# 32-column tiles for attention values and row sums, a bank of their own for the sums, and a new placing of the surrounding matmuls

## The chip, the cores and the metric

The kernel runs on one core of one Trainium2 chip. The metric is device time in microseconds (us) of one execution. The median of several executions is quoted, with the lowest and highest. Engines are named as in the profile: PE (matmuls), PEld (weight loads, overlapping PE), DVE (VectorE), ACT (ScalarE), POOL (GpSimd), SP (SyncE). Where the text says "wait", the next instruction in the engine's order could not start yet. An instruction that is ready can also stand behind others that the program issued before it on its engine; the profile before shows a case of 1.5 us.

## The reference, cut to what matters

Attention over 8 batches of 8 heads (576 tokens, 64 channels per head, 16 extra "beacon" keys that everybody sees, otherwise causal), then a gated feed-forward block on the result:

```python
# q, k, v: (8, 8, 576, 64); beacon_k, beacon_v: (8, 8, 16, 64)
scores = scale * q @ concat(beacon_k, k).T        # causal on the 576 own keys
a = exp(scores - max); a /= a.sum(-1)
x = (a @ concat(beacon_v, v))                     # -> (4608, 512), heads side by side
out = (gelu(x @ w_gate) * (x @ w_val)) @ w_out    # 512 -> 1536 -> 512
```

## The kernel before: the parts that matter

Heads go in pairs (4 pairs per batch, m = 0 to 3). For each pair, scores come in four chunks: a and b, then c and d, each into one of two "scores" tiles of PSUM (`psum_s`, two buffers), from where ACT takes the exponential. "Attend" multiplies the exponentials with the values, and with a block of ones for the row sums. The feed-forward gates of a batch follow, as one block of 96 matmuls; the output matmuls (48 per batch, index u) of the *previous* batch are spread between the attention steps of the next one, to give PE something to do while ACT works. (The feed-forward runs in nine chunks of 512 tokens; the last two come after the last batch.) Twelve output matmuls accumulate one output tile, which DVE then copies out of PSUM.

```python
psum_s: 2 buffers of 2 banks;  psum_x: 1 buffer of 3 banks;  psum_o: 1 buffer of 1 bank

def attend(b, m, t, wide=False):         # two column tiles: head 0 and head 1, 64 columns each
    ...
    for w, (ps, base, split) in enumerate(x_of[i]):      # w=0: values, w=1: sums
        for q0, q1 in ...:
            for hi in range(2):
                mm(ps[64*hi : 64*hi+64, base+q0 : base+q1],
                   ones[0:kr, :] if w else v_sb[0:kr, t, 2*m+hi, :],
                   expT[0:kr, hi, e0 : e0+q1-q0], ...)

def normalize(b, m, by_act=False, direct=False):
    ...
    act(x_sb, x_ps, ACT.Copy)                             # values out of PSUM (not if direct)
    keep(nc.vector.transpose(zT_sb, z_ps))                # 128 x 576
    keep(nc.vector.reciprocal(r_sb, ...))                 # 128 x 18
    keep(nc.vector.transpose(rec_sb, r_sb spread))        # 128 x 576
    keep(nc.vector.tensor_tensor(out=xT_sb[...], in0=x_sb, in1=rec_sb, op=ALU.mult))

def out_mms(ci, u0, u1, wide):
    for u in range(u0, u1):
        ti, fi = divmod(u, 12)
        if fi == 0:       # a new output tile: tile 0 in psum_x, tiles 1 to 3 in the one bank psum_o
            o_ps = psum_x.tile(...) if wide(ti) else psum_o.tile(...)
        mm(o_ps, ...)
        if fi == 11:
            keep(nc.vector.tensor_copy(o_sb[:, ti, :], o_ps)); ...   # and the store

# one batch, from the second on (o(n): the next n output matmuls of the batch before)
o(6);  ab(0);  o(10);  cd(0);  o(8)
for m in 1, 2, 3:
    ab(m);  av(m - 1);  cd(m);  o(6 if m < 3 else 5)      # av = attend, then normalize
av(3);  o(7)
... 96 gate matmuls ...
```

`keep` pins an instruction to its place in the program's order on its engine.

The softmax here doesn't subtract the row's maximum and nothing guards it: scores larger than these inputs give would overflow.

## Time and profile before

398.44 us, median of 3 runs (398.13 to 399.09).

| | before |
|---|---|
| span in the profile | 396.2 us |
| PE busy | 382.3 us, 97% |
| ACT / DVE / POOL busy | 51% / 48% / 39% |
| granted PE clock | full (1.00) |
| one steady batch | 42.2 us |

From the page of the kernel before, part 1, and the two rows of part 2 for PE and its clock (the span in 40 slices, each digit tenths):

```profile
PE 382.3 (97%) x3046; PEld 185.9 (47%) x3046; DVE 190.5 (48%) x304; ACT 202.2 (51%) x280; POOL 156.3 (39%) x277
...
PE   3889999999999999999999999999999999999996
...
PEclk9999999999999999999999999999999999999999
```

Only the first slices and the last are not full. Busy time alone would not prove that PE is the limit, but the list of what PE waited for does (columns: who waited, for whom, total us, how often, longest us). These are all of its lines:

```profile
PE t_ps L167 <- DMA qk_103<-in_q_dram: 4.4, 1, 4.4
PE s_ps L155 <- DVE qkT L183: 1.5, 1, 1.5
PE x_ps L155 <- DVE zT_sb L304: 1.1, 1, 1.1
PE s_ps L155 <- ACT expT L158: 1.0, 2, 0.8
PE gv_ps L155 <- DVE xT_sb L312: 0.8, 1, 0.8
PE x_ps L155 <- DVE x_sb L297: 0.4, 1, 0.4
PE t_ps L167 <- DVE qkT L183: 0.4, 2, 0.2
PE t_ps L167 <- DMA qk_103<-in_k_dram: 0.2, 1, 0.2
PE s_ps L155 <- DMA qkT<-k_sb_94: 0.2, 1, 0.2
```

Nearly all of it is in the first 32 us. After that the kernel is a stream of PE work with no hole worth speaking of.

The timeline of the kernel before around the end of an output tile, DVE and the next output matmul only (columns: start us, duration us, engine, line, operation, tiles, shapes, count):

```profile
111.79 0.78 DVE L307 STREAM_TRANSPOSE rec_sb<-r_sb 128x576 f32<-128x576 f32 x1
...
112.60 0.76 DVE L312 TENSOR_TENSOR xT_sb<-x_sb,rec_sb 128x576 bf16<-128x576 f32 x1
...
113.28 0.68 DVE L364 COPY o_sb<-o_ps 128x512 f32<-128x512 f32 x1
...
114.37 0.61 PE L155 MATMUL o_ps<-wo_sb,hT_sb 128*128 128x512 bf16 x2
```

The output tile that is copied at 113.28 got its last matmul from 111.43 to about 111.8. The copy began 1.5 us after that, behind the transposes and the multiply of a normalization that the program issued before it. In this kernel that did no harm, because the group of output matmuls ended with that tile, and the next one started at 114.37, 0.4 us after the copy's end.

The c/d scores that follow an attend, from their start to the next output matmul (PE only):

```profile
105.78 0.60 PE L155 MATMUL s_ps<-qkT 64*128 64x464 bf16 x4
106.32 1.47 PE L155 MATMUL o_ps<-wo_sb,hT_sb 128*128 128x512 bf16 x6
```

That is 0.54 us, against 0.39 us for the c/d scores of pair 0, which have ten output matmuls before them.

### The profile page before, as it was taken

To read this page: it belongs to the slowest core of one execution; us is meant where nothing else is said; L and a number is where in the kernel's file an instruction comes from. 1 tells how busy PE (TensorE), PEld (TensorE's weight loads), DVE (VectorE), ACT (ScalarE), POOL (GpSimd) and SP (SyncE) were. 2 spreads that over 40 slices of the span, in tenths; PEclk is the share of its full clock that TensorE was granted. 3 is DMA by queue.
4 is the path that set the end of the run, shared out by engine and by line. 5 is a ranking of instruction groups with operands and counts; after the bars stand their busy time and mean duration, and the time that the engine had idled before them with its cause. 6 is when DMAs were issued, how large, how long until landed. Compare 5 with 4: busy or idle time off the path is not lost.

```text
span 396.2 us, 7413 instructions
## 1 busy us (share of the span) xinstructions
PE 382.3 (97%) x3046; PEld 185.9 (47%) x3046; DVE 190.5 (48%) x304; ACT 202.2 (51%) x280; POOL 156.3 (39%) x277
## 2 busy tenths in 40 slices
PE   3889999999999999999999999999999999999996
PEld 2464545544454445444544455444544455444442
DVE  1393654844375327642673338433754266332332
ACT  2775258634873379336843586347823793332210
POOL 8722395780369124931486047803400240000000
PEclk9999999999999999999999999999999999999999
DMA  7999998699129930996099915991032010000012
GB/s 91 180 206 204 175 132 97 68 169 121 55 36 156 141 79 30 120 156 84 29 107 162 89 55 57 163 137 58 28 89 59 34 45 32 0 0 29 28 53 106
DMA packets 139154, 36.24 MB, mean 91 GB/s; under 512 B 126832, under 2 KB 134512, under 8 KB 139120
## 3 DMA queue, kind: packets, MB, share of 16 engines
q0 software_dynamic: 103984, 19.14, 64.4%
q1 hardware_dynamic: 35136, 16.62, 19.3%
q8 instruction: 24, 0.39, 0.4%
q14 instruction: 10, 0.08, 0.1%
HBM read 38.27 MB, written 9.44 MB: 120 GB/s over the span
## 4 chain that ended last, share of the span: by engine, by line
PE 79%; DMA 8%; POOL 3%; DVE 3%; ACT 3%; issue 2%; SPq 2%; POOLq 0%; ACTq 0%
PE gv_ps L155 36%; PE o_ps L155 23%; PE x_ps L155 11%; PE s_ps L155 8%; DMA qkT<-k_sb_94 3%; DMA v_sb_98<-in_beacon_v_dram 2%; SPq L196 2%; ACT expT L158 2%; DMA k_sb_97<-in_k_dram 2%; POOL k_sb_97 L109 1%; PE t_ps L167 1%; DVE qkT L178 1%; POOL q_sb_96 L109 1%; PE w_ps L155 1%; DMA kb<-in_beacon_k_dram 1%
## 5 line engine op out<-in xcount | busy, mean ns | idle before, releaser
L158 ACT ACTIVATE ge_sb<-gv_ps 128x512 bf16<-128x512 f32 x108 | 64.5, 597 | 150.7 <-PE gv_ps L155 150.7
L340 DVE TENSOR_TENSOR hT_sb<-gv_ps,ge_sb 128x512 bf16<-128x512 f32 x108 | 74.7, 692 | 116.0 <-ACT ge_sb L158 116.0
L158 ACT ACTIVATE expT<-s_ps 128x1024 bf16<-128x1024 f32 (+3 forms) x128 | 103.9, 870 | 25.8 <-PE s_ps L155 25.7
L155 PE MATMUL gv_ps<-xT_sb,wg_sb 128*128 128x512 bf16 x432 | 112.2, 379 | 0.8 <-DVE xT_sb L312 0.8
L155 PE MATMUL gv_ps<-xT_sb,wv_sb 128*128 128x512 bf16 x432 | 112.2, 379 | 0.0
L238 POOL TENSOR_SCALAR_AFFINE_SELECT expT<-expT 128x256 bf16<-128x256 bf16 (+2 forms) x140 | 52.4, 388 | 142.2 <-ACT expT L158 142.1
L155 PE MATMUL o_ps<-wo_sb,hT_sb 128*128 128x512 bf16 x432 | 103.6, 380 | 0.0
L155 PEld LDWEIGHTS <-wv_sb 128*128 128x128 bf16 x432 | 42.3, 98 | 52.7 <-issue 2.7
L155 PEld LDWEIGHTS <-wg_sb 128*128 128x128 bf16 x432 | 41.9, 98 | 49.9
L155 PEld LDWEIGHTS <-hT_sb 128*128 128x128 bf16 x432 | 38.8, 98 | 46.6 <-issue 2.8
L364 DVE COPY o_sb<-o_ps 128x512 f32<-128x512 f32 x36 | 24.7, 687 | 37.9 <-PE o_ps L155 37.9
L155 PE MATMUL s_ps<-qkT 64*128 64x80 bf16 (+5 forms) x384 | 39.1, 294 | 2.7 <-DVE qkT L183 1.5
L155 PE MATMUL x_ps<-expT,ones 128*64 128x432 bf16 (+1 forms) x558 | 41.2, 243 | 0.0
L304 DVE STREAM_TRANSPOSE zT_sb<-x_ps 128x576 f32<-128x576 f32 x29 | 22.7, 781 | 29.9 <-ACT x_sb L158 29.9
L155 PEld LDWEIGHTS <-qkT 64*128 64x128 bf16 x384 | 14.8, 96 | 30.4 <-issue 21.8
L155 PEld LDWEIGHTS <-ones 128*64 128x64 bf16 (+1 forms) x578 | 23.2, 110 | 4.6
L307 DVE STREAM_TRANSPOSE rec_sb<-r_sb 128x576 f32<-128x576 f32 x29 | 22.6, 778 | 1.0
L155 PE MATMUL x_ps<-expT,v_sb_95 128*64 128x80 bf16 (+5 forms) x270 | 21.5, 245 | 1.5 <-DVE zT_sb L304 1.1
L155 PE MATMUL x_ps<-expT,v_sb_98 128*64 128x80 bf16 (+5 forms) x288 | 22.8, 246 | 0.0
L109 POOL DMA_DIRECT2D v_sb_98<-in_v_dram x20 | 17.0, 868 | 11.9 <-DMA wv_sb<-in_moe_w_val_dram 3.7
L109 POOL DMA_DIRECT2D v_sb_95<-in_v_dram x20 | 17.0, 889 | 2.5 <-DMA k_sb_94<-in_k_dram 2.3
L312 DVE TENSOR_TENSOR xT_sb<-x_sb,rec_sb 128x576 bf16<-128x576 f32 x23 | 17.4, 758 | 0.9
(51 smaller groups left out, 190.9 us busy)
## 6 DMA issues: line engine op xcount, KB each, us to landing
out_dram<-o_sb SPq DMA_DIRECT2D x36, 256.0 KB, 2.0
v_sb_95<-in_v_dram POOLq DMA_DIRECT2D x12, 128.0 KB, 7.9
wg_sb<-in_moe_w_gate_dram POOLq DMA_DIRECT2D x3, 512.0 KB, 11.6
wv_sb<-in_moe_w_val_dram POOLq DMA_DIRECT2D x3, 512.0 KB, 13.3
wo_sb<-in_moe_w_out_dram POOLq DMA_DIRECT2D x1, 1536.0 KB, 23.5
v_sb_98<-in_v_dram POOLq DMA_DIRECT2D x12, 128.0 KB, 10.6
q_sb_93<-in_q_dram POOLq DMA_DIRECT2D x12, 128.0 KB, 4.2
q_sb_96<-in_q_dram POOLq DMA_DIRECT2D x12, 128.0 KB, 4.2
```

Of the source, the lines that this page charges most:

```text
L109: keep(nc.gpsimd.dma_start(out=out_ap, in_=in_ap))
L155: keep(nc.tensor.matmul(out_ap, lhsT, rhs, start=start, stop=stop, **kw))
L158: keep(nc.scalar.activation(out_ap, in_ap, func, **kw))
L167: keep(nc.tensor.transpose(out_ap, in_ap, ident[0:n, 0:n]))
L178: nc.vector.tensor_copy(qkT[:, m, :, NB:SK].rearrange("p w (t r) -> p w t r", r=6), t_ps[:, 0:2, 0:S].rearrange("p w (r t) -> p w t r", r=6),)
L196: nc.sync.dma_start_transpose(out=qkT[:, :, w, c + j * P : c + j * P + n], in_=src[0:n, j, :, :].rearrange("p h d -> p (h d)"),)
L238: nc.gpsimd.affine_select(out=d, in_=d, pattern=[[0, 2], [1, n]], compare_op=ALU.is_ge, fill=0.0, base=NB if t == 0 else 0, channel_multip ...
L304: keep(nc.vector.transpose(zT_sb, z_ps))
L307: nc.vector.transpose(rec_sb.rearrange("p (c o) -> p c o", o=32), r_sb.to_broadcast([P, S // 32, 32]))
L312: nc.vector.tensor_tensor(out=xT_sb[:, m, b * S : (b + 1) * S], in0=x_sb, in1=rec_sb, op=ALU.mult)
L340: nc.vector.tensor_tensor(out=h_of[ci][:, fi, :], in0=gv_ps[:, 1, :], in1=ge_sb, op=ALU.mult)
L364: keep(nc.vector.tensor_copy(o_sb[:, ti, :], o_ps))
```

## The change

Its intent: the row sums do not need 64 copies per head. With 32-column tiles, four tiles fit side by side in the array, so two query ranges (0 to 352 and 352 to 576) of both heads are summed at once: 960 streamed columns instead of 1664. Values use 32-column tiles too (same streamed columns), so that the shape of the array does not change within an attend; heads then interleave over groups of 32 rows, and the gate weights are loaded in that order. Sums come first and go to a bank of their own (`psum_z`), so DVE can start on them while the values still stream; the multiply reads the values from PSUM, which saves ACT the copy (0.66 us each in the trace before). The last two gate tiles are computed as a pair, gates first, so that ACT is done early. The output matmuls are placed anew.

```diff
+    psum_z = ...(name="psum_z", bufs=1, PSUM)          # one bank; psum_x shrinks to two
     def load_gate_val(i):                              # 24 weight loads instead of 6
+            for g in range(4): ... dst[32*g : 32*g+32] <- rows of (half, head) g
     def attend(b, m, x_in, by_act):
+            z_ps = psum_z.tile([P, 512], FP32, ...)
+            for t, u in Z_ORDER:                       # u: query range
+                for hi in range(2):
+                    p0 = 64 * u + 32 * hi
+                    mm(z_ps[p0 : p0 + 32, ...], ones[0 : KROWS[t], 0:32], expT[...], ...)
+        x_ps = pool.tile([P, 1024], FP32, ...)
+                for r in range(4):
+                    mm(x_ps[32*r : 32*r+32, ...], v_sb[..., 2*m + r%2, 32*(r//2) : 32*(r//2)+32],
+                       expT[..., r % 2, ...], ...)
     def normalize(b, m, by_act):
-            if not direct: act(x_sb, x_ps, ACT.Copy)
-            keep(nc.vector.transpose(zT_sb, z_ps))
-            keep(nc.vector.reciprocal(r_sb, ...))
+            keep(nc.vector.transpose(zT_sb[:, 0:w], z_ps[:, 0:w]))             # 128 x 224
+            keep(nc.vector.transpose(zT_sb[0:64, w:ZS], z_ps[0:64, w:ZS]))     # 64 x 128
+            ... four reciprocals of 64 partitions ...
     def out_mms(...):
-                    o_ps = psum_x.tile(...)             # tile 0 (tiles 1 to 3: psum_o, as before)
+                    o_ps = psum_z.tile(...)
+    def gate_val_pair(ci, f0): ... # gates of both tiles, then values of both
     # one batch
-            o(6);  ab(0);  o(10);  cd(0);  o(8)
-            for m: ab(m); av(m-1); cd(m); o(6 if m < NPAIR - 1 else 5)
-            av(3, direct=True);  o(7)
+            o(4);  ab(0);  o(6);   cd(0);  o(4)
+            for m: ab(m); av(m-1); cd(m); o(8)
+            av(3);  o(10)
```

More of the change, by code (lines that the diff above doesn't have):

```diff
@@ L38 @@
 AV_ORDER = [0, 2, 4, 1, 3]
-X0 = 16
-Z0 = X0 + S
+X0 = 512 - S_LO[4]
+ZS = 352
+Z_ORDER = [(0, 0), (0, 1), (1, 1), (1, 0), (2, 1), (2, 0), (3, 1), (4, 1)]
 QK_SCALE = 0.125
@@ L77 @@
     psum_x = ctx.enter_context(tc.tile_pool(name="psum_x", bufs=1, space=bass.MemoryType.PSUM))
+    psum_z = ctx.enter_context(tc.tile_pool(name="psum_z", bufs=1, space=bass.MemoryType.PSUM))
     psum_o = ctx.enter_context(tc.tile_pool(name="psum_o", bufs=1, space=bass.MemoryType.PSUM))
@@ L148, in load_gate_val @@
         for w, dst in ((moe_w_gate, wg_sb), (moe_w_val, wv_sb)):
-            keep(nc.gpsimd.dma_start(out=dst[:, :, fs], in_=w[:, fs].rearrange("(kk p) f -> p kk f", p=P)))
+            for g in range(4):
+                a, c = g % 2, g // 2
+                dma(
+                    dst[32 * g : 32 * g + 32, :, fs],
+                    w[:, fs].rearrange("(kk q p) f -> q p kk f", q=4, p=32)[2 * a + c],
+                )
     def load_out_w():
@@ L161, in transpose_pe @@
     def transpose_pe(b, m, pool, tag):
-        t_ps = pool.tile([P, 3 if tag == "x" else 2, 1024], BF16, name="t_ps", tag=tag)
+        t_ps = pool.tile([P, 2, 1024], BF16, name="t_ps", tag=tag)
         qk, kb = qk6[b]
@@ L251, with attend @@
     x_of = {}
-    def attend(b, m, t, wide=False):
+    def attend(b, m, x_in, by_act):
         i = b * NPAIR + m
-        if t == AV_ORDER[0]:
-            if wide:
-                x_of[i] = tuple(
-                    (psum_s.tile([P, 1024], FP32, name=name, tag="s"), 0, 512) for name in ("xs_ps", "zs_ps")
-                )
-            else:
-                x_ps = psum_x.tile([P, 1536], FP32, name="x_ps", tag="x")
-                x_of[i] = ((x_ps, X0, 512 - X0), (x_ps, Z0, 1024 - Z0))
-        expT, v_sb = exp_of[i], v_ring[b % NRING]
-        kr, first, last = KROWS[t], t == AV_ORDER[0], t == AV_ORDER[-1]
-        for w, (ps, base, split) in enumerate(x_of[i]):
-            for q0, q1 in ((S_LO[t], split), (max(split, S_LO[t]), S)):
+        expT, v_sb = exp_of[i], v_ring[b % NRING]
+        if by_act:
+            z_ps = psum_s.tile([P, 1024], FP32, name="z_ps", tag="s")
+            for t in AV_ORDER:
+                for q0, q1 in ((S_LO[t], 512), (max(512, S_LO[t]), S)):
+                    e0 = EXP_OFF[t] + q0 - S_LO[t]
+                    for r in range(4):
+                        mm(
+                            z_ps[32 * r : 32 * r + 32, q0:q1],
+                            ones[0 : KROWS[t], 0:32],
+                            expT[0 : KROWS[t], r % 2, e0 : e0 + q1 - q0],
+                            t == AV_ORDER[0],
+                            t == AV_ORDER[-1],
+                            skip_group_check=True,
+                        )
+        else:
+            z_ps = psum_z.tile([P, 512], FP32, name="z_ps", tag="z")
+            for t, u in Z_ORDER:
+                lo, end = (ZS, S) if u else (0, ZS)
+                q0 = max(lo, S_LO[t])
+                e0 = EXP_OFF[t] + q0 - S_LO[t]
+                for hi in range(2):
+                    p0 = 64 * u + 32 * hi
+                    mm(
+                        z_ps[p0 : p0 + 32, q0 - lo : end - lo],
+                        ones[0 : KROWS[t], 0:32],
+                        expT[0 : KROWS[t], hi, e0 : e0 + end - q0],
+                        t == 0,
+                        t == (4 if u else 2),
+                        skip_group_check=True,
+                    )
+        pool, tag = x_in
+        x_ps = pool.tile([P, 1024], FP32, name="x_ps", tag=tag)
+        for t in AV_ORDER:
+            for q0, q1 in ((S_LO[t], S_LO[4]), (max(S_LO[4], S_LO[t]), S)):
@@ L269, in attend @@
                 e0 = EXP_OFF[t] + q0 - S_LO[t]
-                for hi in range(2):
+                for r in range(4):
                     mm(
-                        ps[64 * hi : 64 * hi + 64, base + q0 : base + q1],
-                        ones[0:kr, :] if w else v_sb[0:kr, t, 2 * m + hi, :],
-                        expT[0:kr, hi, e0 : e0 + q1 - q0],
-                        first and (wide or not (w == 1 and q0 == 0)),
-                        last,
+                        x_ps[32 * r : 32 * r + 32, X0 + q0 : X0 + q1],
+                        v_sb[0 : KROWS[t], t, 2 * m + r % 2, 32 * (r // 2) : 32 * (r // 2) + 32],
+                        expT[0 : KROWS[t], r % 2, e0 : e0 + q1 - q0],
+                        t == AV_ORDER[0],
+                        t == AV_ORDER[-1],
@@ L277, in attend, with normalize @@
                         skip_group_check=True,
                     )
-    def normalize(b, m, by_act=False, direct=False):
+        x_of[i] = x_ps[:, X0 : X0 + S], z_ps
+    def normalize(b, m, by_act):
         i = b * NPAIR + m
-        (x_ps, xc, _), (z_ps, zc, _) = x_of.pop(i)
-        x_ps, z_ps = x_ps[:, xc : xc + S], z_ps[:, zc : zc + S]
+        x_ps, z_ps = x_of.pop(i)
         del exp_of[i]
         rec_sb = npool.tile([P, S], FP32, name="rec_sb", tag="rec_sb")
-        x_sb = x_ps
-        if not direct:
-            x_sb = npool.tile([P, S], FP32, name="x_sb", tag="x_sb")
@@ L293, in normalize @@
         if by_act:
-            ln_sb = npool.tile([P, S], FP32, name="ln_sb", tag="zT_sb")
-            act(ln_sb, z_ps, ACT.Ln)
-            if not direct:
-                keep(nc.vector.tensor_copy(x_sb, x_ps))
+            ln_sb = npool.tile([P, S], FP32, name="ln_sb", tag="ln_sb")
+            act(ln_sb, z_ps[:, 0:S], ACT.Ln)
             act(rec_sb, ln_sb, ACT.Exp, scale=-1.0)
         else:
-            zT_sb = npool.tile([P, S], FP32, name="zT_sb", tag="zT_sb")
+            zT_sb = npool.tile([P, ZS], FP32, name="zT_sb", tag="zT_sb")
@@ L301, in normalize @@
             r_sb = npool.tile([P, S // 32, 1], FP32, name="r_sb", tag="r_sb")
-            if not direct:
-                act(x_sb, x_ps, ACT.Copy)
-            keep(nc.vector.transpose(zT_sb, z_ps))
-            keep(nc.vector.reciprocal(r_sb, zT_sb.rearrange("p (c o) -> p c o", o=32)[:, :, 0:1]))
+            n, w = ZS // 32, S - ZS
+            keep(nc.vector.transpose(zT_sb[:, 0:w], z_ps[:, 0:w]))
+            keep(nc.vector.transpose(zT_sb[0:64, w:ZS], z_ps[0:64, w:ZS]))
+            z = zT_sb.rearrange("p (c o) -> p c o", o=32)[:, :, 0:1]
@@ L306, in normalize @@
+            for p in (64, 0):
+                keep(nc.vector.reciprocal(r_sb[p : p + 64, n:, :], z[64:P, 0 : w // 32, :]))
+            for p in (0, 64):
+                keep(nc.vector.reciprocal(r_sb[p : p + 64, 0:n, :], z[0:64, :, :]))
             keep(
@@ L312, in normalize @@
             nc.vector.tensor_tensor(
-                out=xT_sb[:, m, b * S : (b + 1) * S], in0=x_sb, in1=rec_sb, op=ALU.mult
+                out=xT_sb[:, m, b * S : (b + 1) * S], in0=x_ps, in1=rec_sb, op=ALU.mult
             )
@@ L318, with feed_tile, gv_mm, gelu @@
     h_of, o_of = {}, {}
-    def gate_val(ci, fi, kk_late=False):
+    def feed_tile(ci, fi):
         if fi == 0:
             h_of[ci] = hpool.tile([P, F_TILES, CH], BF16, name="hT_sb", tag="hT_sb")
-        n0 = ci * CH
-        gv_ps = psum_s.tile([P, 2, CH], FP32, name="gv_ps", tag="s")
-        order = [(w, kk) for w in range(2) for kk in range(K_CHUNKS)]
-        if kk_late:
-            order.sort(key=lambda t: t[1] == K_CHUNKS - 1)
-        for w, kk in order:
-            mm(
-                gv_ps[:, w, :],
-                (wg_sb, wv_sb)[w][:, kk, fi * P : (fi + 1) * P],
-                xT_sb[:, kk, n0 : n0 + CH],
-                kk == 0,
-                kk == K_CHUNKS - 1,
-                skip_group_check=True,
-            )
+        return psum_s.tile([P, 2, CH], FP32, name="gv_ps", tag="s")
+    def gv_mm(gv_ps, ci, fi, w, kk):
+        mm(
+            gv_ps[:, w, :],
+            (wg_sb, wv_sb)[w][:, kk, fi * P : (fi + 1) * P],
+            xT_sb[:, kk, ci * CH : (ci + 1) * CH],
+            kk == 0,
+            kk == K_CHUNKS - 1,
+            skip_group_check=True,
+        )
+    def gelu(gv_ps):
         ge_sb = fpool.tile([P, CH], BF16, name="ge_sb", tag="ge_sb")
         act(ge_sb, gv_ps[:, 0, :], ACT.Gelu)
+        return ge_sb
+    def product(ci, fi, gv_ps, ge_sb):
         keep(
@@ L343, in gate_val, with gate_val_pair @@
         )
+    def gate_val(ci, fi, kk_late=False):
+        gv_ps = feed_tile(ci, fi)
+        order = [(w, kk) for w in range(2) for kk in range(K_CHUNKS)]
+        if kk_late:
+            order.sort(key=lambda t: t[1] == K_CHUNKS - 1)
+        for w, kk in order:
+            gv_mm(gv_ps, ci, fi, w, kk)
+        product(ci, fi, gv_ps, gelu(gv_ps))
+    def gate_val_pair(ci, f0):
+        tiles = [feed_tile(ci, f0), feed_tile(ci, f0 + 1)]
+        ge = []
+        for i, gv_ps in enumerate(tiles):
+            for kk in range(K_CHUNKS):
+                gv_mm(gv_ps, ci, f0 + i, 0, kk)
+            ge.append(gelu(gv_ps))
+        for i, gv_ps in enumerate(tiles):
+            for kk in range(K_CHUNKS):
+                gv_mm(gv_ps, ci, f0 + i, 1, kk)
+            product(ci, f0 + i, gv_ps, ge[i])
     def out_mms(ci, u0, u1, wide=lambda ti: False):
@@ L351, in out_mms @@
                 if wide(ti):
-                    o_of[ci][1] = psum_x.tile([P, 1536], FP32, name="o_ps", tag="x")[:, 0:D_MODEL]
+                    o_of[ci][1] = psum_z.tile([P, D_MODEL], FP32, name="o_ps", tag="z")
                 else:
@@ L404, in cd, with av @@
             scores(b, m, 3)
-        def av(m, wide=False, **kw):
-            for t in AV_ORDER:
-                attend(b, m, t, wide)
-            normalize(b, m, **kw)
+        def av(m, by_act=False, x_in=(psum_x, "x")):
+            attend(b, m, x_in, by_act)
+            normalize(b, m, by_act)
         keep(nc.scalar.preload_act_table_set(SET_EXP))
@@ L433 @@
             av(1, by_act=True)
-            av(2, wide=True, by_act=True, direct=True)
-            av(3, by_act=True, direct=True)
-        else:
-            o(6)
-            ab(0)
-            o(10)
+            av(2, by_act=True, x_in=(psum_s, "s"))
+            av(3, by_act=True)
+        else:
+            o(4)
+            ab(0)
+            o(6)
             cd(0)
-            o(8)
+            o(4)
             for m in range(1, NPAIR):
@@ L445 @@
                 cd(m)
-                o(6 if m < NPAIR - 1 else 5)
-            av(3, direct=True)
-            o(7)
+                o(8)
+            av(3)
+            o(10)
         keep(nc.scalar.preload_act_table_set(SET_GELU))
         for fi in range(F_TILES):
-            gate_val(b, fi, kk_late=fi == 0)
+            if fi < F_TILES - 2:
+                gate_val(b, fi, kk_late=fi == 0)
+            elif fi == F_TILES - 2:
+                gate_val_pair(b, fi)
             if b == 0 and 6 <= fi < 10:
```

## The prediction

> **What bounds it now.** The page has PE busy 97% of a 396.2 us span, clock full. PE hardly waits (view of waits: 10 us, nearly all in the first 32 us). A steady batch is one PE stream: gates 20.8 us, then 21.4 us to the next gates (chain of waits). In the timeline a 512-column matmul takes 217 ns; two 64-column tiles start 3 ns apart and together take columns/2.4 ns (432 columns: 180 ns). [...]
>
> **What the change does to PE.** Values: four 32-column tiles instead of two of 64, same 1664 streamed columns per head pair, the same time. Sums: 1664 columns become 960 (two query ranges side by side): -704 columns = -0.29 us per head pair, for 29 of 32: -8.5 us if four tiles overlap as two do. The 36 matmuls of a head pair take 1.56 us now; the new 52 about 1.27.
>
> **Why I do not expect that gain.**
> 1. After scores a/b, PE does the attend, then scores c/d, whose second half needs the exp of b to be done: 2.42 us after the phase began. PE already waits 0.13 us there (464-column score: 334 instead of 204 ns to the next). An attend shorter by 0.29 us only lengthens this wait. Three of four attends per batch gain nothing; cd(0), now after 6 output matmuls instead of 10, waits about 0.3 us too. Little of the gain is left.
> 2. The output matmuls are redistributed: groups ended at 6, 16, 24, 30, 36, 41, 48; now at 4, 10, 14, 22, 30, 38, 48. Output tiles change at 12, 24, 36. Tiles 1 to 3 share the single bank psum_o, so matmul 24 must wait for the VectorE copy of tile 1, and 36 for that of tile 2. Before, groups ended at 24 and 36 and other work followed; now these lie inside a group. The copy stands behind the normalization of the same phase in VectorE's order: already in before one copy started 1.5 us late, right behind the multiply.
>    Sums are ready 1.16 us into the phase; VectorE then needs transposes of 224 and 128 columns (estimated from 781 ns for 576: 0.45+0.35), four small reciprocals (1.0, from 267 ns for one of 18), transpose 0.81, multiply 0.76, copy 0.69: matmul 24 or 36 starts about 5.3 us into its phase. Without the wait: 3.1 and 3.9 us. Waits: 2.2 + 1.4 us per batch, x 7: 25 us.
>
> Per batch 21.4 becomes about 24.9 us: +24 us in all. The copy removed from ACT (22 x 0.66 us) and the early gates shorten what is not the limit; batch 0 about 0.
>
> **Predicted: 421 us, range 410 to 430. Faster by over 2%: 0.04; within 2%: 0.11; slower by over 2%: 0.85.**
>
> **What would show it.** PE waits on the VectorE copy into o_sb, two per batch, 1 to 2.5 us each, 20 to 28 us in total; PE's busy share falling to about 91%; sums of one head pair streaming in about 0.4 us, attend in about 1.27 us; scores waiting about 0.4 us on exp; ACT busy down 14 us, VectorE up about 15 us.
>
> **What would make it wrong.** The copy running ahead of the normalization: then 395 to 400 us. Four tiles not overlapping (issue-bound at 80 columns, 8 instructions per 33 ns): later still.

That four tiles overlap as two do was the assumption; the trace before shows it for two (starts 3 ns apart).

## The result, and the profile after

431.55 us, median of 4 runs (430.15 to 432.54), against 398.28 us (397.48 to 399.09) of the kernel before. Ratio of the fast runs 1.083, 95% interval 1.079 to 1.087. A ratio is the mean time of one kernel's fast runs over that of the other's fast runs of the same rounds, so it is not quite the ratio of the medians. Every run counted here is fast (a run is called slow when it is over 1.5% above the fastest of its kernel). The direction was predicted; the size was not: 33 us lost where 23 us were forecast, and 431.55 us lies above the stated range.

From the page of the changed kernel, the same parts:

```profile
PE 378.6 (88%) x3576; PEld 184.9 (43%) x3626; DVE 200.9 (47%) x419; ACT 190.4 (44%) x258; POOL 165.0 (38%) x295
...
PE   3879997899789997999789978999699978999996
...
PEclk9999999999999998999899998999999989999999
```

PE has less to do (378.6 us) in a longer span (429.1 us; 50 of its 3626 matmul records are missing from this trace, so the 88% is a little low), and there is something new in the last row: four slices with a granted clock below full. What PE waited for, the longest totals:

```profile
PE o_ps L166 <- DVE o_sb L420: 19.7, 14, 1.8
PE s_ps L166 <- ACT expT L169: 5.8, 20, 0.8
...
PE gv_ps L166 <- DVE hT_sb L374: 3.8, 7, 0.5
...
PE x_ps L166 <- DVE xT_sb L344: 1.4, 1, 1.4
```

Fourteen waits for the copy into o_sb: two in each of seven batches. The timeline of one of them, DVE and output matmuls only:

```profile
113.11 0.42 DVE L331 STREAM_TRANSPOSE zT_sb<-z_ps 128x224 f32<-128x224 f32 x1 [1.27 <-PE z_ps L166]
113.45 0.26 DVE L332 STREAM_TRANSPOSE zT_sb<-z_ps 64x128 f32<-64x128 f32 x1
...
113.75 0.41 DVE L335 RECIPROCAL r_sb<-zT_sb 64x7 f32<-64x7 f32 x2
114.17 0.45 DVE L337 RECIPROCAL r_sb<-zT_sb 64x11 f32<-64x11 f32 x2
...
114.66 0.78 DVE L339 STREAM_TRANSPOSE rec_sb<-r_sb 128x576 f32<-128x576 f32 x1
114.80 0.38 PE L166 MATMUL o_ps<-wo_sb,hT_sb 128*128 128x512 bf16 x1 [0.16 <-issue]
...
115.54 0.76 DVE L344 TENSOR_TENSOR xT_sb<-x_ps,rec_sb 128x576 bf16<-128x576 f32 x1
116.21 0.68 DVE L420 COPY o_sb<-o_ps 128x512 f32<-128x512 f32 x1
...
116.94 1.46 PE L166 MATMUL o_ps<-wo_sb,hT_sb 128*128 128x512 bf16 x6 [1.77 <-DVE o_sb L420]
```

The matmul at 114.80 completes an output tile. The next one needs the same bank, so it needs the copy; the copy stands behind the whole normalization, and PE resumes at 116.94. Of this wait, 1.04 us is the late start of the copy (the matmul ends at 115.17, the copy starts at 116.21) and the rest is the copy itself. At matmul 36 of the same batch the copy starts only 0.17 us late, so there the wait is nearly all copy.

The c/d scores after an attend, now with a visible wait for the exponential:

```profile
109.27 0.37 PE L166 MATMUL s_ps<-qkT 64*128 64x464 bf16 x2
109.92 0.27 PE L166 MATMUL s_ps<-qkT 64*128 64x208 bf16 x2 [0.28 <-ACT expT L169]
```

They take 0.84 us to the next output matmul, whose record is one of the missing ones.

And the clock. Stretches of the changed kernel (columns: stretch, its length, busy us of PE, PEld, DVE, ACT, POOL with counts, granted PE clock, DMA share, GB/s), first in a batch where the clock fell:

```profile
159.16:162.57 3.41, 1.35 (x27) 0.66 (x19) 3.20 (x9) 2.17 (x4) 1.88 (x5) 1.00 0.00 0
162.57:165.98 3.41, 3.27 (x12) 1.05 (x13) 0.09 (x1) 0.00 (x0) 0.00 (x0) 0.50 0.23 82
165.98:169.40 3.42, 3.05 (x67) 1.97 (x63) 2.38 (x8) 3.31 (x5) 1.60 (x5) 1.00 0.00 0
```

and in a batch where it did not:

```profile
114.78:118.19 3.41, 1.62 (x7) 0.58 (x6) 2.01 (x3) 0.79 (x2) 1.11 (x4) 1.00 0.13 49
```

The trace's record of the granted clock changes in steps of 3.41 us. After a step in which PE was busy for 1.35 us of 3.41, the next step ran at half the clock: 512-column matmuls started 427 ns apart in it, against 217 ns elsewhere. That happened in 4 of 7 batches in this execution, after steps with 1.2 to 1.4 us of PE work. In the three batches without it the emptiest step held 1.6, 1.6 and 2.0 us. The number of half-clock steps differs between executions: the mean clocks of the four runs are 0.984, 0.976, 0.984 and 0.980, and the two runs with the lower clocks are the two longest.

Where the 32.9 us between the two profiled spans went, from the starts of single instructions in the two traces:

| part | before | after | difference |
|---|---|---|---|
| start to the end of batch 0's gates (how sure this is: under "Why the prediction was wrong") | 55.3 us | 56.6 us | +1.3 us |
| a batch at full clock | 42.2 us | 45.8 us | +3.6 us, 7 times: +25 us |
| 4 batches with a half-clock step | | 47.3 us | +1.5 us, 4 times: +6 us |
| the rest (second batch's start, end) | | | +0.6 us |

Within a batch (a wait is counted here from start to start of the two output matmuls, less the usual 0.217 us):

| stage | before | after |
|---|---|---|
| 96 gate matmuls | 20.83 us | 21.43 us |
| attend of each of the 4 pairs | 1.56 us | 1.25 us |
| c/d scores of pairs 1 to 3 | 0.54 us | 0.84 us |
| c/d scores of pair 0 | 0.39 us | 0.69 us |
| wait inside the output matmuls | none | 1.93 + 1.07 us |

These differences add up to the +3.6 us: 0.6 - 1.24 + 0.9 + 0.3 + 3.0.

### The profile page after: what moved, and what is told of

It is laid out like the page before. It is cut to its first block, busy times and chain, and to the rows that moved or that the text cites. A ratio compares the mean times of both kernels' runs of the same rounds, so it can differ in the third digit from the quotient of the medians.

```text
span 429.1 us, 8701 instructions
## 1 busy us (share of the span) xinstructions
PE 378.6 (88%) x3576; PEld 184.9 (43%) x3626; DVE 200.9 (47%) x419; ACT 190.4 (44%) x258; POOL 165.0 (38%) x295
## 3 DMA queue, kind: packets, MB, share of 16 engines
q0 software_dynamic: 104272, 19.15, 58.2%
## 4 chain that ended last, share of the span: by engine, by line
PE 63%; DVE 13%; DMA 8%; ACT 6%; POOL 5%; issue 3%; DVEq 0%; ACTq 0%; POOLq 0%
PE gv_ps L166 37%; PE o_ps L166 18%; ACT expT L169 5%; PE s_ps L166 4%; DMA wo_sb<-in_moe_w_out_dram 4%; PE z_ps L166 3%; DVE rec_sb L339 3%; DVE xT_sb L344 2%; DVE o_sb L420 2%; DMA v_sb<-in_v_dram 2%; PE x_ps L166 2%; DVE r_sb L337 1%; POOL v_sb L114 1%; DVE zT_sb L331 1%; DVE r_sb L335 1%
## 5 line engine op out<-in xcount | busy, mean ns | idle before, releaser
L169 ACT ACTIVATE expT<-s_ps 128x1024 bf16<-128x1024 f32 (+3 forms) x128 | 101.4, 865 | 58.7 <-PE s_ps L166 58.7
L166 PEld LDWEIGHTS <-wg_sb 128*128 128x128 bf16 x432 | 41.8, 98 | 55.1 <-issue 6.1
L166 PE MATMUL s_ps<-qkT 64*128 64x80 bf16 (+5 forms) x384 | 42.0, 303 | 8.2 <-ACT expT L169 5.8
L114 POOL DMA_DIRECT2D v_sb<-in_v_dram x40 | 33.9, 881 | 7.1 <-DMA k_sb<-in_k_dram 3.1
L331 DVE STREAM_TRANSPOSE zT_sb<-z_ps 128x224 f32<-128x224 f32 x29 | 12.1, 417 | 48.0 <-PE z_ps L166 48.0
L166 PE MATMUL x_ps<-expT,v_sb 128*32 128x80 bf16 (+5 forms) x1152 | 32.5, 244 | 2.1 <-DVE xT_sb L344 1.4
L166 PEld LDWEIGHTS <-v_sb 128*32 128x32 bf16 (+1 forms) x1152 | 28.3, 97 | 3.0 <-issue 2.5
L114 POOL DMA_DIRECT2D q_sb<-in_q_dram x30 | 25.3, 857 | 7.1 <-DMA wo_sb<-in_moe_w_out_dram 6.5
L344 DVE TENSOR_TENSOR xT_sb<-x_ps,rec_sb 128x576 bf16<-128x576 f32 x32 | 24.2, 758 | 6.1 <-PE x_ps L166 1.6
L114 POOL DMA_DIRECT2D k_sb<-in_k_dram x30 | 25.4, 893 | 0.4 <-DMA q_sb<-in_q_dram 0.3
L166 PE MATMUL z_ps<-expT,ones 128*32 128x224 bf16 (+10 forms) x584 | 21.1, 256 | 1.2 <-POOL expT L249 0.6
```

The lines of the kernel that those rows point to most:

```text
L114: keep(nc.gpsimd.dma_start(out=out_ap, in_=in_ap))
L166: keep(nc.tensor.matmul(out_ap, lhsT, rhs, start=start, stop=stop, **kw))
L169: keep(nc.scalar.activation(out_ap, in_ap, func, **kw))
L331: keep(nc.vector.transpose(zT_sb[:, 0:w], z_ps[:, 0:w]))
L344: nc.vector.tensor_tensor(out=xT_sb[:, m, b * S : (b + 1) * S], in0=x_ps, in1=rec_sb, op=ALU.mult)
```

## The experiments

The theory after this reading, A: the loss is the wait of output matmuls 24 and 36 for a copy that stands behind a normalization, *plus* half-clock steps that these waits cause; the shorter sums earn almost nothing because the c/d scores then wait for the exponential. The rivals: B, the 32-column tiles themselves (or the gate pair) cost the time and pull the clock down; C, the wait is the copy and the reuse of the bank as such, not the place of the copy in DVE's order.

All kernels below gave correct results. Each is compared with the kernel before, run in the same rounds on the same chip (medians 397.96, 398.45 and 398.15 us in the three sets).

### The old counts in the changed kernel

```diff
-            o(4);  ab(0);  o(6);   cd(0);  o(4);   ... o(8), o(8), o(8);  av(3);  o(10)
+            o(6);  ab(0);  o(10);  cd(0);  o(8);   ... o(6), o(6), o(5);  av(3);  o(7)
```

> The changed kernel with the output-matmul counts of the kernel before (6, 10, 8, then 6, 6, 5, and 7), so that the groups end at 24 and 36 again. Theory A (the loss is matmuls 24 and 36 waiting inside a group for the VectorE copy, plus the half-clock windows that follow): the 20 us of PE waits on o_sb go, no half-clock window is left, batch 45.8 -> about 42.5 us, time about 402 us. Rival B (the 32-column tiles, or the gate pair, cost it): stays above 420 us, half-clock windows stay.

Measured: 401.66 us (400.23 to 402.95), ratio 1.008. This placing alone takes back 30 of the 33 us. Waits of PE in this kernel (`a_counts`), the first two lines:

```profile
PE s_ps L166 <- ACT expT L169: 6.7, 23, 0.8
PE t_ps L178 <- DMA qk<-in_q_dram: 4.8, 1, 4.8
```

The waits for o_sb are in none of its lines. One half-clock step is left, in the first 30 us, where PE waits for other things; none in the batches (mean granted clock of this profile 0.996, of the other three runs 1.000). A batch is 42.65 us. Rival B falls: the 32-column tiles and the gate pair are all there. The attend takes 1.25 us and the c/d scores 0.84 us, so what the sums gave (0.31 us) the wait for exp took (0.30 us).

### The new counts in the kernel before

```diff
-            o(6);  ab(0);  o(10);  cd(0);  o(8);   ... o(6), o(6), o(5);  av(3);  o(7)
+            o(4);  ab(0);  o(6);   cd(0);  o(4);   ... o(8), o(8), o(8);  av(3);  o(10)
```

> The kernel before with nothing but the counts of the changed one (4, 6, 4, 8, 8, 8, 10). Theory A: slower than the changed kernel, since here the normalization ends later (copy of values and sums last): matmul 24 about 6.4 us into its phase, 36 the same, 5.7 us of waits per batch, some half-clock windows; 438 to 450 us. Rival B: about 398 to 402 us.

Measured: 461.33 us (460.96 to 462.14), ratio 1.159. This is the old kernel with nothing but the placing of existing matmuls changed. It was expected to be worse than the changed kernel, and is, by more than expected:

```profile
PE o_ps L155 <- DVE o_sb L364: 37.6, 14, 3.1
```

Waits are twice those of the changed kernel. The program shows why the normalization ends later here: the sums end together with the values, and ACT copies the values first. In the trace the two copies of the batch shown below start 2.33 and 1.59 us after their tile's last matmul, against 1.04 and 0.17 us. The part that was underrated is again the clock: this profile has a half-clock stretch in each of seven batches, two steps long in six of them (one batch has two single ones); its mean granted clock is 0.948. Stretches of one batch:

```profile
118.37:121.79 3.42, 1.34 (x18) 0.54 (x13) 2.25 (x4) 2.28 (x4) 1.57 (x5) 1.00 0.00 0
121.79:125.20 3.41, 2.42 (x6) 0.69 (x5) 0.93 (x2) 0.00 (x0) 0.00 (x0) 0.50 0.23 82
125.20:128.61 3.41, 3.41 (x35) 1.99 (x36) 0.00 (x0) 1.89 (x2) 0.91 (x3) 0.50 0.00 0
128.61:132.02 3.41, 2.25 (x24) 0.98 (x19) 2.08 (x4) 2.85 (x4) 1.39 (x4) 1.00 0.00 0
```

Fourteen steps of 3.41 us at half clock cost at most half of that each, 24 us by this estimate; with 6 us of waits per batch (5.4 for the copies and about 0.6 elsewhere) that is the measured 63 us, within 5%.

### PE kept busy through the waits

```diff
     def o(n):
+            for _ in range(n):
+                if u[0] in (24, 36):          # just before the matmul that will wait
+                    f_ps = psum_z.tile([P, D_MODEL], FP32, name="f_ps", tag="z")
+                    for _ in range(8 if u[0] == 24 else 4):
+                        mm(f_ps, ident, qkT[:, 3, 1, 0:512], True, True)   # result unused
                 ... then one output matmul at a time
```

> The changed kernel with 8 and 4 idle matmuls into the sums' bank just before matmuls 24 and 36 (same work at the same places, PE busy while it would wait). Theory A2 (the half clock is a reaction to PE waiting): no half-clock window, 5 to 6 us faster than the changed kernel, about 426 us. Rival (the clock falls for another reason, such as the load of four tiles): half-clock windows stay, 431 us or more.

Measured: 425.70 us (425.07 to 426.29), ratio 1.070: 5.9 us less than the changed kernel, although PE does 84 matmuls more. A batch takes 45.8 us, as in the changed kernel's batches at full clock, and no batch after the first has a half-clock step (batch 0 has one, at 31 us, after other waits; mean granted clock 0.996). So the waits cost their own length, and the slow clock is a second cost that they bring about. That the four-tile work alone lowers the clock is ruled out: it is all there.

### The copy on another engine

```diff
-                keep(nc.vector.tensor_copy(o_sb[:, ti, :], o_ps))
+                if ci < N_CHUNKS - 2 and ti in (1, 2):
+                    act(o_sb[:, ti, :], o_ps, ACT.Copy)
+                else:
+                    keep(nc.vector.tensor_copy(o_sb[:, ti, :], o_ps))
```

> The changed kernel with the copies of output tiles 1 and 2 done by ACT, which has no normalization in its queue. Theory A (the copy is late because it stands behind the normalization): matmul 24 starts at about 4.45 us of its phase in place of 5.2, matmul 36 at about 4.75 us; 1.3 us per batch less, no half-clock window; 414 to 418 us. Rival C (the wait is the copy itself, 0.7 us, and the bank's reuse): unchanged, 431 us.

Measured: 417.47 us (416.20 to 418.13), ratio 1.048: 14 us less than the changed kernel. The same tile, bank and matmuls, with no normalization ahead of the copy (but ACT's exponentials: at matmul 24 the copy still starts 0.26 us late):

```profile
PE o_ps L166 <- ACT o_sb L169: 11.3, 14, 0.9
```

The waits shrink from 1.8 to at most 0.9 us, and no half-clock step is left in the trace (mean granted clock 1.000). A batch is 44.7 us, 1.1 us less than the changed kernel's 45.8: about 7.5 us in seven batches, and about 6 us are the half clock. Rival C holds for the rest: with the bank reused inside a group, a wait of about a copy's length stays, and the kernel is still 16 us slower than with the old counts. So the place in DVE's order is about a third of the waiting (1.1 of 3.0 us per batch) and, with the half clock that goes with it, 14 of the 30 us; the change of tile inside a group is the rest.

### Without the gate pair

```diff
-            if fi < F_TILES - 2: gate_val(b, fi, kk_late=fi == 0)
-            elif fi == F_TILES - 2: gate_val_pair(b, fi)
+            gate_val(b, fi, kk_late=fi == 0)
```

(on top of the old counts; label `a_nopair`)

> The changed kernel with the counts of before and without the gate pair (the last two gate tiles as all others). Theory: the pair makes its second tile wait 0.5 us for a bank of PSUM, 0.6 us per batch in the gates (21.43 against 20.83 us), and its early exp is worth nothing with 10 output matmuls behind scores a/b: 4 us less than with the pair (401.7), so about 397.5 us. Rival (the pair pays by an earlier start of exp): 402 us or more.

Measured: 396.92 us (396.46 to 397.67), ratio 0.996. The pair cost 4.7 us (5.2 us when each of the two kernels is taken against the kernel before in its own rounds). The timeline of the changed kernel shows how, PE and DVE lines at the pair:

```profile
98.77 1.03 PE L166 MATMUL gv_ps<-xT_sb,wg_sb 128*128 128x512 bf16 x4
...
99.60 0.69 DVE L374 TENSOR_TENSOR hT_sb<-gv_ps,ge_sb 128x512 bf16<-128x512 f32 x1 [1.03 <-ACT ge_sb L169]
...
100.34 1.02 PE L166 MATMUL gv_ps<-xT_sb,wg_sb 128*128 128x512 bf16 x4 [0.55 <-DVE hT_sb L374]
```

Computing the gates of both tiles first means that the second tile is asked for after 4 matmuls instead of 8, while its buffer still holds the tile before the pair.

### Work between scores and attend

If the c/d scores wait for exp because the attend became shorter, something must be put in between.

```diff
+            o(6);  ab(0);  o(10);  cd(0);  o(6)
+            for m in 1, 2, 3:
+                ab(m);  o(2);  av(m - 1);  cd(m);  o(4 if m < 3 else 6)
+            av(3);  o(6)
```

(label `a_two`, without the gate pair; output tiles end at 24 and 36, each followed by an attend, and the copy is issued ahead of that attend's normalization)

> As a_nopair, but two output matmuls between scores a/b and the attend (counts 6, 10, 6, then 2+4, 2+4, 2+6, and 6; tiles end at group ends 24 and 36 before the attend). Theory (the shorter sums were swallowed by the wait of the last score on exp, 0.84 us against 0.54 for the c/d scores): c/d back to 0.39 us without a wait, attend 1.25 us, 1.3 to 1.4 us per batch less than before, 388 to 391 us. Rival (the exp wait moves with the work, or the added change of tile shape costs as much): 396 us or more.

Measured: 395.04 us (393.56 to 395.63), ratio 0.991. The c/d scores are back at 0.39 us, as expected, but the total fell by 1.9 us, not by 6 to 9. Part of the wait seems to have moved: the a/b scores of pairs 2 and 3 now take 0.72 us instead of 0.53, with only four output matmuls before them to give ACT time for c/d (the list of waits shows none there, so this reason is not shown), and the fourth attend takes 1.74 us, since its values wait for the multiply of the third (`psum_x` has one buffer).

The control `b_two`, the same placing in the kernel before:

> The kernel before with the same placing of output matmuls as a_two: control for how much of a_two's gain is the placing alone. Theory: only the 0.15 us of exp wait per phase goes and a change of shape of 0.1 us comes: 396 to 398 us. Rival (the placing is the gain): below 393 us.

The trace before shows the change of shape that this expects: from the start of the last score (80 columns) to that of the first value matmul it is 126 ns, from an 80-column value matmul to the next matmul of the same attend 32 ns.

Measured: 405.46 us (404.15 to 406.63), ratio 1.018. This expectation was wrong, in a useful way. In the old kernel the placing makes things worse: the a/b scores wait for ACT, which there still has the copy of values (0.65 us) to do between two exponentials. From the timeline of this control, ACT and scores:

```profile
107.50 0.65 ACT L158 ACTIVATE x_sb<-x_ps 128x576 f32<-128x576 f32 x1 [0.36 <-PE x_ps L155]
...
108.05 2.50 ACT L158 ACTIVATE expT<-s_ps 128x928 bf16<-128x928 f32 x3
...
109.04 0.80 PE L155 MATMUL s_ps<-qkT 64*128 64x512 bf16 x8 [0.21 <-ACT expT L158]
```

So with this placing the changed attention is 10.4 us faster than the old one; with the old placing it was 1.5 us faster (`a_nopair` against its own kernel before). Per batch the difference is 1.5 us (43.2 against 41.7). The shorter attends of pairs 0 to 2 are 0.9 us of that; how much the removed copy gives was not tested apart. Against the old kernel with its own placing the gain is 0.9%.

### Two attempts to take the remaining waits away

The fourth pair's values in a scores tile, on top of `a_two` (label `a_three`):

```diff
-            av(3)
+            av(3, x_in=(psum_s, "s"))
```

> As a_two, with the values of the fourth head pair of batches 1 to 7 in a scores bank, so that they need not wait for the multiply of the third (attend of the fourth pair 1.74 us in a_two, 1.25 without a wait). Theory: 0.49 us x 7 = 3.4 us less than a_two (395.0), about 391.6 us, 1.7% under the kernel before. If the wait only moves (second gate tile waiting for that bank): as a_two.

Measured: 393.67 us (392.67 to 394.25, 5 runs), ratio 0.988 (0.986 to 0.990), the best of all. 1.4 us of the 3.4 came: the fourth attend went from 1.74 to 1.46 us, not to 1.25. What is left is a gap of about 0.2 us in the middle of its sums, before the matmul over the fourth block of keys: POOL ends its mask over that block at 116.08 us, and the matmul starts at 116.13. One phase of this kernel (PE only), from the a/b scores to the next output matmul:

```profile
107.41 0.79 PE L166 MATMUL s_ps<-qkT 64*128 64x512 bf16 x8
108.13 0.61 PE L166 MATMUL o_ps<-wo_sb,hT_sb 128*128 128x512 bf16 x2
108.67 0.56 PE L166 MATMUL z_ps<-expT,ones 128*32 128x352 bf16 x14
...
109.92 0.46 PE L166 MATMUL s_ps<-qkT 64*128 64x464 bf16 x4
110.31 0.39 PE L166 MATMUL o_ps<-wo_sb,hT_sb 128*128 128x512 bf16 x1
```

Batch 0 was aimed at twice, by giving the second attend's values a scores tile:

```diff
-            av(1, by_act=True)
-            av(2, by_act=True, x_in=(psum_s, "s"))
+            av(1, by_act=True, x_in=(psum_s, "s"))
+            av(2, by_act=True)
```

once on `a_two` with 16 instead of 24 weight loads (i = 1 and 2 in one; label `a_best`):

> As a_two, with 16 in place of 24 weight loads and, in batch 0, the second attend's values in a scores bank so that they need not wait 1.4 us for the multiply of the first. 1 to 2 us less than a_two if these two were what made batch 0 about 1.9 us longer than before; the same as a_two if not.

Measured: 397.05 us; one of its four runs, the profiled one, was slow (409.04 us, granted clock 0.947) and does not count; the three fast ones are 396.77 to 397.08 us, ratio 0.996: 2 us *more* than `a_two`. Its three fast runs have a mean clock of 0.996, as one half-clock step gives in other runs here, and the profiled run has such a step at 32 us, after a pause of 3.1 us; so the clock may be where the 2 us went. And once alone on `a_three` (label `a_four`):

> As a_three, with the second attend's values of batch 0 in a scores bank (the other half of a_best, without its merged weight loads). Its wait of 0.9 us for the first multiply goes: about 1 us less than a_three, 390.6 us. If the pause without a semaphore in batch 0 (0.7 us in the changed kernel, 3.1 us in a_best) takes it back: as a_three or 1 to 2 us more.

Measured: 394.43 us (393.02 to 396.19), ratio 0.991: no gain in the median. The six runs fall in two groups: three of 393.0 to 393.5 us with clocks of 0.998 or 0.999, and three of 395.4 to 396.2 us with 0.994 or 0.995, about one half-clock step less. So half of the executions seem to have paid for a slow step. In the profile the wait for the multiply fell from 1.4 to 0.2 us, and another pause grew, which the profile puts down to nothing it can see:

```profile
29.29 0.31 PE L166 MATMUL x_ps<-expT,v_sb 128*32 128x80 bf16 x11 [1.82 <-issue]
```

This pause stands before the same eleven matmuls in the changed kernel (0.70 us) and in seven of its eight variants, in the middle of an accumulation where no semaphore is waited for. It is 0.7 to 2.0 us long in kernels whose program is the same up to there, so that it grew here because of the edit is not shown. In the old counts, where a half-clock step made PE come later (29.70 us), there is no pause. The DMA records of the changed kernel's trace: the queue that the profile page calls "instruction" (q8) brings 16384 bytes from 27.55 to 28.44 us, with the DMA engines busy 90% or more throughout 24 to 32 us, and PE goes on at 29.99 us, 1.55 us after that packet's end. That the pause has to do with this packet is not shown, and no run tests it.

## Why the prediction was wrong, point by point

The direction (slower by over 2%) and its main mechanism were right. The sum was too small, by 10.6 us (421 against 431.55). The step that failed is the clock: the sum takes it as full throughout, and the runs show about 6 us of half clock that the waits bring about.

- *"Sums ... -0.29 us per head pair"*, attend about 1.27 us: right, 1.25 us against 1.56. Four 32-column tiles overlap as two of 64 do: their starts lie 3 to 4 ns apart in the trace after (two of 64: 3 ns).
- *"An attend shorter by 0.29 us only lengthens this wait"*: right. The old counts in the changed kernel show 0.84 us for the c/d scores against 0.54.
- *"Waits: 2.2 + 1.4 us per batch"*: the mechanism was right, shown by the counts in both kernels; the copy on ACT shows that the normalization ahead of the copy is about a third of the waiting and the copy inside the group the rest. The size was 1.93 + 1.07 us. The normalization, from the first transpose to the end of the multiply, takes 3.2 us, not 3.4 (the 64-partition transpose 0.26 us for 0.35, the reciprocals about 0.2 us each).
- *"the early gates shorten what is not the limit"*: wrong. They lengthen what is: 0.6 us per batch, 4.7 us in the run without the pair. The prediction looked at what the pair does for ACT and not at when its second tile needs a buffer.
- *"Per batch 21.4 becomes about 24.9 us: +24 us in all"*: +3.6 us per batch at full clock, 25 us. That this is so near is luck: the last two errors, 0.6 us each, cancel.
- *"clock full"*: this is the step that failed, and the largest of the terms missing. The prediction read the clock of the old kernel and carried it over to a kernel with waits of 2 us in it. It had no term for a clock that falls because PE waits. That term is 5.9 us by the experiment that kept PE busy, and 6 us by the profile. In the old kernel with the new counts it is up to 24 us, more than a third of the loss.
- *"batch 0 about 0"*: +1.3 us in these two profiles. But batch 0 is the same program in the changed kernel and in `a_counts`, `a_fill` and `a_actcopy`, and its end lies at 56.6, 57.1, 58.2 and 55.1 us in their profiles, against 55.3 to 55.6 us in the three of the old kernel. So about 1 us is what can be said. The second attend's wait for the first one's multiply (1.4 us here, 0.9 to 1.6 us in the others) and the pause of 0.7 us lie in it; how it divides was not settled, and taking the wait away gained nothing.

The busy times moved as forecast in sign: ACT down 12 us (14 forecast), DVE up 10 us (15 forecast), PE at 88% (91% forecast).

With those two terms (6 for the clock, about 2 for batch 0 and the ends) the forecast would have been about 429 us.

## What to carry to other kernels

When one accumulation bank is reused within a run of matmuls, ask where its evacuation (the copy that empties it) stands in the evacuating engine's order: put the change of tile at the end of a group of matmuls, with other PE work behind it, and issue the copy ahead of any long chain on that engine (here the old counts took back 30 of 33 us). Faster work on the busiest engine gains only where its next dependency is already fulfilled (here 0.31 us of shorter sums went into 0.30 us of longer wait); otherwise it has to be moved, together with something to fill the place. And when a change adds waits to a matmul stream, count them twice: their length, and the clock they may cost afterwards (here 3.0 us per batch, 21 us in all, and about 6 us).

## What else the traces show of the clock and of the tiles

- The clock record of the changed kernel changes in steps of 3.41 us. The PE records covered 35% to 41% (1.20 to 1.41 us) of each of the four steps in the batches that were followed by a drop from full to half clock; so steps that were only partly idle sufficed, with waits for the copy of at most 1.8 us. The emptiest steps of the other three batches had 48%, 48% and 58%, and no drop followed. In the old kernel with the new counts, the step with 39% (1.34 us) that is shown above was followed by a drop. What decides between 41% and 48% was not tested.
- The four half-clock steps of the changed kernel held 96% to 100% of PE work, and full clock followed each. In the stretches shown of the old kernel with the new counts, a half-clock step with 71% (2.42 us) was followed by a second one; that one held 100%, and full clock followed.
- 52 matmuls of 32 columns in four tiles, 2624 columns deep along the longest tile, took 1.25 us with the change of tile shape in the changed kernel, that is 1.09 us of streaming at 2.4 columns per ns (an estimate from the 180 ns that 432 columns took in the old kernel) and 0.16 us more.
